# Three plain chunks and six by seven products in the last stage, and earlier sums of the last weights' quarters

## The chip, the cores and the metric

One core of one Trainium2 chip runs the kernel. The metric is the time of one execution in microseconds (us) on the device, the median of several runs. Engine names: PE is TensorE, ACT is ScalarE, DVE is VectorE, POOL is GpSimd, SP is SyncE, which here only issues DMAs.

## What is computed

Memory attention for 4 batches, 8 heads, 576 tokens gives 2304 tokens of 512 features. Two feed-forward blocks follow, and the change lies in the second matmul of the second:

```python
x = (x @ w_a) * (x @ w_b) @ w_out          # first block, d_ff = 1536
h = x @ w_in                               # second block, d_ff = 2048
g = h * (1.0 / (1.0 + np.exp(-1.702 * h)))
return g @ w_out                           # 2304 x 2048 by 2048 x 512, float32
```

## The kernel before

**Precision.** Matmuls run on float32 data cut into a high part, which ScalarE makes by a copy with rounding, and a low part, which VectorE or GpSimd makes by subtracting the high one (`hi_lo`, lines 342 to 346). Each product is three passes: high by high, low by high, high by low (`PASSES`, line 18).

**Seven products.** Most matmul stages multiply two-by-two blocks with seven products (P1 to P7) in place of eight. Each product takes one block of the left side, or a sum of blocks, and one of the right side, and the results are added up afterwards. `PRODUCTS` (line 1063) names the operands; the right side's sums of four quarter blocks are T1 to T4.

**The last stage**, `g @ w_out`, begins at 550.67 us. The gated rows g lie in DRAM (`g2d`), transposed, and the 2304 tokens are cut into nine chunks of 256 (`NW`). Chunks 0 to 2 (`NF`) are computed together, interleaved, by plain products (`proj2`, lines 1467 to 1488): for each quarter of the 2048 contraction rows, for each of six sub-tiles of 128 tokens, four 128-row pieces by three passes, 512 columns each. So 72 matmuls make a quarter. Chunk 3 (from `NF` up to `NQ` = `NS` = 4) follows by plain products alone, two sub-tiles. Chunks 4 to 8 go through `proj2_seven` (lines 1496 to 1521): for each product in the order P4, P1, P2, P5, P7, P6, P3 (`LAST`), two halves (`h`) of the contraction rows, each four pairs of row pieces by three passes, 256 columns each.

**Left side.** `load_gated` (line 1359) issues the loads of g from DRAM on SP: quarters of a chunk of 512 KB into the slots `f_s` (the twelve of chunks 0 to 2, then the four of chunk 3), then halves of 1024 KB into the slots `fw_s`, which use the same memory and are given out once all quarters are split (the mark `"front"`, line 1194). `split_gated` (line 1377) makes high and low parts of each quarter and sub-tile in one of six slots `sb_s`; PE's use of a slot gives it back. For a seven-product chunk `sums_gated` (line 1410) also makes the sums S1 to S4 and splits seven operands a half into the same six slots.

**Right side.** The 16 pieces (128 x 512) of `w_out` come in as raw 64-bit words and are decoded: two ACT instructions and one on DVE (lines 437 to 446). Then ACT copies the high part (line 460), ACT's queue stores the decoded rows in DRAM (`w2d`, line 461) and DVE or POOL makes the low part (line 463). The plain products need piece c = 4q to 4q + 3 in quarter q. The seven products need sums of quarters too: `load_pair` (line 1438) reads two row pieces back from `w2d` on ACT's queue, makes four sums of 128 x 256 in place, one after the other, the last being T4, and splits each (`split_t`, line 1463). There are eight pairs. Two slots for them (`tb_s`, line 1184) exist from the start, and the two raw buffers join once everything is decoded (line 1193).

**What sets the order.** The program is straight-line per engine; the order of instructions on each engine and queue is fixed beforehand by a small planner (`Order`, lines 105 to 192). The work is written as streams with a rank (a lower number goes first). Each stream asks for an engine with a start time and a length, or waits for a mark (a planned time) or a slot; the planner takes the request that can start first, and the lower rank among equals. On the chip each engine then runs in this order and waits by semaphores for the data alone. So an engine whose next instruction, or whose next DMA issue, waits holds everything behind it. `PT` = 28 is the rank of the pair streams, `PR` = 30 that of the decodes of `w_out`; the gated splits have 4 and the gated sums 5. In line 1450 a pair's sums wait, in the planner, for the mark `"decoded"`, which line 1192 sets after the last low part of `w_out`:

```python
t = max((yield "mark", "pair", p), (yield "mark", "decoded"))
```

`proj2_seven` waits, for its first chunk, for the marks of all pairs (lines 1498 to 1500).

Of the kernel before, what the change touches and what calls it, by code (L numbers as in the profile page):

```python
# [22 lines left out]
W1 = 0.0  # L23
HOLD = {}
PR = 30
PT = 28
MBN = 8
PA = 10
HOLDD = {4: ("attn", 1, 0)}
# [42 lines left out]
def short():  # L72
    Lengths.dve, Lengths.act, Lengths.psum = 68, 94, 52
    Lengths.pool, Lengths.both, Lengths.slow = 1.0, 1.0, 1.0
# [121 lines left out]
def tile_mem_attention_moe_moe2(  # L196
# [18 lines left out]
    NT, DM = out.shape  # L215
    F1 = w_o1.shape[0]
    F2 = w_o2.shape[0]
    P = 128
# [19 lines left out]
    K4 = F2 // P // 4  # L238
    NB = 2 * P
# [109 lines left out]
    loaded = {}  # L349
# [62 lines left out]
    decoded = {}  # L412
# [350 lines left out]
    def give(slots_, views):  # L763
        slots_.free += [[x, now()] for x in views]
# [296 lines left out]
    A11, A12, A22, S1, S2, S3, S4 = range(7)  # L1061
# [11 lines left out]
    win_s, hb_s, f_s, fw_s, sb_s, tb_s = Slots(), Slots(), Slots(), Slots(), Slots(), Slots()  # L1073
    wo2_t, blocks = {}, []

    def views(m, n, count, o=0):
        return [m[:, o + i * n:o + (i + 1) * n] for i in range(count)]
# [82 lines left out]
    def room_chunks(*flat):  # L1160
        for x in flat:
            od.mark(now(), "room", "o2", len(wo2))
            wo2.append(x.rearrange("p (i f) -> p i f", i=2))
# [4 lines left out]
    def room_last():  # L1168

        short()  # L1170
        od.handicap[DVE] = W1
        room_chunks(*views(big["w1b"], CN, 2, 3 * CN))
        for x, o, n in (
            (big["w1b"], 5 * CN, 4), (attn_m[0], 0, 9), (p2_rest[0], 0, 5), (attn_m[1], 4 * CN, 1),
            (big["w1"], 0, 14),
        ):
            blocks.extend(x.rearrange("p (i f) -> p i f", i=2) for x in views(x, BN, n, o))
        for q in order:
            for j in range(2):
                for u in range(2):  # L1180
                    yield "mark", "g2", q, j, u
        n = KD * 2 * N2
        give(f_s, views(acc, FN, 1, n + 2 * FN))
        give(tb_s, views(acc, 2 * DM, 2))
        for p in range(F2 // P // 2):
            od.spawn(PT, load_pair(p))
        for c, x in enumerate(views(acc, FN, 2, n), len(pieces) - 3):
            yield "mark", "raw", c
            give(f_s, [x])
        t = yield "mark", "wo2", F2 // P - 1  # L1190
        crowded()
        od.mark(t, "decoded")
        give(tb_s, [x[0].rearrange("p f j -> p (f j)").bitcast(F32) for x in raw_t])
        yield "mark", "front"
        wide = views(acc, 2 * FN, 3, n)
        give(fw_s, wide[:2])
        yield "mark", "sw", NQ, 0, A22
        give(fw_s, wide[2:])
        for p in range(F2 // P // 2):
            yield "mark", "wt", p  # L1200
        short()
        give(fw_s, views(acc, 2 * FN, 1))
        for x in raw_t:
            give(dm_s, views(x[0].rearrange("p f j -> p (f j)").bitcast(F32), DM, 2))
# [133 lines left out]

    NF, NQ, NS, NW = 3, 4, 4, NT // NB

    def gated_part(s, i, o, e):
        t = 0.0
# [9 lines left out]
        loaded["f", i, o] = s, f  # L1354

    QUARTERS = [(i, o) for o in range(0, 4 * K4, K4) for i in range(NF)]
    QUARTERS += [(i, o) for i in range(NF, NQ) for o in range(0, 4 * K4, K4)]

    def load_gated():
        for i, o in QUARTERS:  # L1360
            s = yield "slot", f_s
            yield from gated_part(s, i, o, o + K4)
        for i in range(NQ, NW):
            for o in (0, 2 * K4):
                s = yield "slot", fw_s
                yield from gated_part(s, i, o, o + 2 * K4)

    def split_part(t, src, *key):
        b = yield "slot", sb_s
        loaded[key] = b  # L1370
        od.spawn(4, split_into(max(t, b[1]), b, src, key))
# [5 lines left out]
    def split_gated():  # L1377
        for i, o in QUARTERS:
            t = yield "mark", "f", i, o
            slot, f = loaded.pop(("f", i, o))  # L1380
            for s in range(2):
                yield from split_part(t, f[:, :, s * P:(s + 1) * P], "sb", i, o, s)
            for s in range(2):
                t = max(t, (yield "mark", "sb", i, o, s))
            f_s.release(slot, t)
        od.mark(t, "front")
        for i in range(NQ, NW):
            yield from (split_whole(i) if i < NS else sums_gated(i))

    def split_whole(i):  # L1390
        for h in (0, 2 * K4):
            t = yield "mark", "f", i, h
            slot, f = loaded.pop(("f", i, h))
            for o in range(0, 2 * K4, K4):
                for s in range(2):
                    yield from split_part(t, f[:, o:o + K4, s * P:(s + 1) * P], "sb", i, h + o, s)
            for o in range(0, 2 * K4, K4):
                for s in range(2):
                    t = max(t, (yield "mark", "sb", i, h + o, s))
            fw_s.release(slot, t)  # L1400

    A21 = 7
    MERGE = {
# [34 lines left out]
    def load_pair(p):  # L1438

        t = max((yield "mark", "w2d", 2 * p), (yield "mark", "w2d", 2 * p + 1))  # L1440
        for x in blocks[4 * p:4 * p + 4]:
            wo2_t.setdefault(p, []).append(x)
        m = yield "slot", tb_s
        x = m[0].rearrange("p (k j f) -> p k j f", k=2, j=2)
        nc.scalar.dma_start(
            out=x.rearrange("p k j f -> p k (j f)"),
            in_=w2d[2 * p * P:(2 * p + 2) * P, :].rearrange("(k p) f -> p k f", p=P),
        )
        od.load(max(t, m[1]), 2 * P * DM * 4, "pair", p)
        t = max((yield "mark", "pair", p), (yield "mark", "decoded"))  # L1450
        b11, b12, b21, b22 = (x[:, k, j] for k in range(2) for j in range(2))
        n = DM // 2
        for i, (dst, in0, in1) in enumerate(
            ((b11, b12, b11), (b12, b22, b12), (b22, b22, b11), (b21, b21, b22))
        ):
            t = yield from combine(t, dst, in0, in1, ALU.subtract, n)
            od.spawn(PT, split_t(t, wo2_t[p][i], dst, p, i))
        for i in range(4):
            t = max(t, (yield "mark", "wt", p, i))
        tb_s.release(m, t)  # L1460
        od.mark(t, "wt", p)
# [33 lines left out]

    def proj2_seven(i):

        if i == NS:
            for p in range(2 * K4):
                yield "mark", "wt", p  # L1500
        ps, ts = {}, {}
        for name in LAST:
            a, b = PRODUCTS[name]
            for h in (0, 2 * K4):
                t = yield "mark", "sw", i, h, a
                x = loaded.pop(("sw", i, h, a))
                if h == 0:
                    t, ps[name] = yield PE, t, 360 * K4, bank_m
                else:
                    t, _ = yield PE, t, 360 * K4  # L1510
                for c in range(K4):
                    for n, (mv, sw) in enumerate(PASSES):
                        nc.tensor.matmul(  # L1513
                            ps[name][0][:, :NB], x[0][:, sw, c, :], moving(b, h // 2 + c, mv),
                            start=(h == c == n == 0), stop=(h > 0 and c == K4 - 1 and n == 2),
                        )
                sb_s.release(x, t)
            ts[name] = t
            od.mark(t, "done", i, name)
            if name == LAST[0]:  # L1520
                od.spawn(0, sums_out(i, ps))
# [65 lines left out]
    def main():  # L1587
        yield from all_gated()
        od.spawn(9, part_again())
        room_gated()  # L1590
        crowded()
        for p in range(NP):
            yield from project(p)
        yield from quad(*order[0])
        od.rate, od.land = 385.0, 2000.0
        room_projected()
        od.spawn(6, load_gated())
        od.spawn(5, split_gated())
        for q in order[1:]:
            yield from quad(*q)  # L1600
            if q == (NG2 - 1, 0):
                room_chunks(*views(eff_m, CN, 6), *views(attn_m[1], CN, 4))
            if q == (NG2 - 1, 1):
                room_split(*views(big["w1"], SN, 6, 14 * WN))
                room_chunks(*views(big["w1"], CN, 1, 14 * WN + 6 * SN), *views(big["w1b"], CN, 3))
        od.spawn(9, room_last())
        yield from proj2([(i, s) for i in range(NF) for s in range(2)])
        for i in range(NF, NW):
            yield from (proj2([(i, 0), (i, 1)]) if i < NS else proj2_seven(i))

    def quad(g, p):
        for name in ("P1", "P6", "P7", "P5", "P3", "P4", "P2"):
# [2 lines left out]
    with tc.manual_schedule():  # L1615
# [19 lines left out]
        for n in range(NU):  # L1635
            p = 10 + n if n >= NHG else 10 + PC * n
# [44 lines left out]
```

## Time and profile before

| | |
|---|---|
| median of three runs | 745.47 us (744.72 to 747.44) |
| profiled execution | 744.51 us |
| span of its instructions | 742.7 us |
| PE busy | 732.1 us, 99% |
| DVE, ACT, POOL busy | 533.2, 430.8, 386.1 us |
| mean granted PE clock | 0.999 of full speed |

The profile is of one execution. Its span runs from the first to the last instruction; 1.81 us of the execution's time lie around it. Busy time of an engine is the sum of its instructions; matmuls overlap each other, so a matmul's own duration is longer than the spacing between two of them. In a row of a group the number behind the bar is the sum in us, then the mean in ns of one instruction, then idle time ahead of them with what ended it. Row texts such as `w<-acc,w` name the output and the inputs by their tiles: `w` is the memory of the six split slots, among others, `acc` that of the loaded chunks, `raw` the raw buffers.

### The profile page before, as it was taken

How to read it: one execution, taken by the hardware profiler on the slowest of the kernel's cores; microseconds unless marked ns; L12 is line 12 of the kernel's file. 1: busy time of each engine (PE TensorE's matmuls, PEld its weight loads, DVE VectorE, ACT ScalarE, POOL GpSimd, SP SyncE). 2: the span in 40 equal slices, each digit the busy share in tenths (PEclk: the TensorE clock that was granted, in tenths of full speed). 3: DMA queues.
4: the chain of work that ended last, by engine and by line, in shares of the span. 5: the costliest groups of instructions: out<-in, count | busy, mean ns of one | idle time of the engine just before them, and what ended most of it. 6: DMA issues, size and time to landing. Idle time of an engine off the chain costs nothing.

```text
span 742.7 us, 14507 instructions
## 1 busy us (share of the span) xinstructions
PE 732.1 (99%) x5344; PEld 682.7 (92%) x5344; DVE 533.2 (72%) x799; ACT 430.8 (58%) x842; POOL 386.1 (52%) x347
## 2 busy tenths in 40 slices
PE   9899999999999999999999999999999999999997
PEld 8787888888889999999999999999998888999997
DVE  2987777568983447945898666666665697898884
ACT  3678664667863456546866655565656654544441
POOL 0324366447996616914998621333240296776660
PEclk9999999999999999999999999999999999999999
DMA  8998954786778966676525575544699954544411
GB/s 276 343 327 254 322 190 160 224 280 231 256 237 264 313 195 170 171 211 191 186 100 163 180 227 162 163 136 150 210 377 301 328 157 138 189 143 143 143 26 33
DMA packets 110359, 153.53 MB, mean 207 GB/s; under 512 B 8400, under 2 KB 89040, under 8 KB 110288
## 3 DMA queue, kind: packets, MB, share of 16 engines
q1 hardware_dynamic: 104928, 143.13, 60.3%
q10 hardware_dynamic: 5360, 9.47, 3.9%
q8 instruction: 42, 0.69, 0.4%
q14 instruction: 29, 0.24, 0.1%
HBM read 100.01 MB, written 52.56 MB: 205 GB/s over the span
## 4 chain that ended last, share of the span: by engine, by line
PE 92%; DMA 3%; POOL 2%; DVE 2%; SPq 1%; issue 0%; ACT 0%; DVEq 0%; POOLq 0%
PE bank L1281 24%; PE bank L844 21%; PE bank L1006 16%; PE bank L1513 14%; PE bank L1482 12%; PE bank L792 3%; DMA q<-in_q_dram 1%; PE bank L590 1%; DMA raw_p<-in_moe_w_b_dram 1%; DMA kv<-in_k_dram 1%; PE bank L509 1%; POOL w L339 1%; SPq L372 1%; POOL attn L339 1%; DVE attn L339 0%
## 5 line engine op out<-in xcount | busy, mean ns | idle before, releaser
L844 PEld LDWEIGHTS bank<-attn,eff 128*128 128x128 f32 x1152 | 154.3, 188 | 16.2 <-issue 6.1
L844 PE MATMUL bank<-attn,eff 128*128 128x288 f32 x1152 | 163.1, 298 | 0.5 <-DVE eff L812 0.5
L339 POOL TENSOR_TENSOR acc<-acc 128x512 f32<-128x512 f32 (+2 forms) x65 | 95.0, 1481 | 68.2 <-DVE w L339 27.9
L1323 DVE TENSOR_TENSOR acc<-bank,acc 128x384 f32<-128x384 f32 x168 | 89.8, 553 | 46.3 <-PE bank L1281 40.8
L339 DVE TENSOR_TENSOR w<-acc,w 128x512 fp32r<-128x512 f32 (+2 forms) x100 | 105.0, 1076 | 20.5 <-ACT w L345 20.4
L345 ACT ACTIVATE w<-acc 128x512 fp32r<-128x512 f32 (+2 forms) x129 | 74.9, 590 | 65.7 <-PE bank L1513 38.9
L345 ACT ACTIVATE attn<-acc 128x768 fp32r<-128x768 f32 (+2 forms) x80 | 61.0, 769 | 54.5 <-PE bank L1006 38.7
L1006 PE MATMUL bank<-attn,w 128*128 128x384 f32 x504 | 91.8, 335 | 0.8 <-DVE attn L339 0.7
L1006 PEld LDWEIGHTS bank<-attn,w 128*128 128x128 f32 x504 | 87.5, 188 | 2.0 <-DVE attn L339 1.4
L339 DVE TENSOR_TENSOR attn<-acc,attn 128x768 fp32r<-128x768 f32 (+2 forms) x54 | 65.6, 1225 | 31.9 <-ACT attn L345 30.8
L1333 ACT ACTIVATE acc<-acc 128x384 f32<-128x384 f32 x96 | 49.3, 524 | 44.0 <-DVE acc L1323 43.0
L339 POOL TENSOR_TENSOR attn<-acc,attn 128x768 fp32r<-128x768 f32 (+2 forms) x26 | 41.9, 1623 | 35.8 <-ACT attn L345 35.8
L1281 PE MATMUL bank<-attn,w 128*128 128x384 f32 x288 | 55.1, 334 | 0.0
L339 POOL TENSOR_TENSOR w<-dm,w 128x256 fp32r<-128x256 f32 x27 | 24.5, 908 | 57.9 <-ACT w L345 57.9
L888 POOL TENSOR_TENSOR gr<-gr 128x288 f32<-128x288 f32 x48 | 44.6, 931 | 17.0 <-issue 7.0
L339 POOL TENSOR_TENSOR w<-acc,w 128x256 fp32r<-128x256 f32 (+2 forms) x27 | 30.0, 1119 | 44.4 <-ACT w L345 44.3
L1281 PEld LDWEIGHTS bank<-attn,w 128*128 128x128 f32 x288 | 50.4, 188 | 0.0
L1006 PE MATMUL bank<-attn,w1b 128*128 128x384 f32 x252 | 47.6, 336 | 0.2 <-DVE attn L339 0.2
L339 POOL TENSOR_TENSOR sT<-sT,sm 128x576 f32<-128x576 f32 (+1 forms) x12 | 13.5, 1126 | 64.0 <-DVE sm L654 31.7
L1281 PE MATMUL bank<-w1b,w 128*128 128x384 f32 x224 | 46.2, 334 | 0.0
L1006 PEld LDWEIGHTS bank<-attn,w1b 128*128 128x128 f32 x252 | 43.8, 188 | 0.9 <-DVE attn L339 0.5
L1281 PE MATMUL bank<-w 128*128 128x384 f32 x224 | 43.8, 334 | 0.0
(185 smaller groups left out, 1448.9 us busy)
## 6 DMA issues: line engine op xcount, KB each, us to landing
acc<-g1d SPq DMA_DIRECT2D x63, 384.0 KB, 3.8
g2d<-acc SPq DMA_DIRECT2D x96, 192.0 KB, 2.0
raw<-in_moe_w_out_dram SPq DMA_DIRECT2D x24, 512.0 KB, 4.9
acc<-g2d SPq DMA_DIRECT2D x10, 1024.0 KB, 7.6
raw<-in_moe_w_in_dram SPq DMA_DIRECT2D x16, 512.0 KB, 4.3
acc<-g2d SPq DMA_DIRECT2D x16, 512.0 KB, 5.5
g1d<-gr SPq DMA_DIRECT2D x12, 576.0 KB, 4.9
g1d<-acc SPq DMA_DIRECT2D x8, 576.0 KB, 4.8
```

The costliest lines, as they stand in the source:

```text
L339: (nc.gpsimd if e == POOL else nc.vector).tensor_tensor(out=dst, in0=in0, in1=in1, op=op)
L345: nc.scalar.activation(out=hi, in_=src, func=AF.Copy)
L372: nc.sync.dma_start(out=dst.rearrange("p (n f) w -> p n (f w)", n=runs), in_=src)
L792: nc.tensor.matmul(ps[c][0][row(h), :], bdv[b][half, h, :], wt["wab", g, h][0][half, :], start=True, stop=True)
L844: nc.tensor.matmul(dst[:, :U], e[:, c, sw, i * CW + j * P:i * CW + (j + 1) * P], attn(b, mv, c, u * U, U), start=(n == 0), stop=(n == 3 * ...
L888: nc.gpsimd.tensor_tensor(out=dst, in0=in0, in1=in1, op=ALU.subtract)
L1006: nc.tensor.matmul(ps[0][:, :N2], w1_of(a, g, sw)[:, r * P:(r + 1) * P], b[0][:, mv, i], start=(first and q == n == 0), stop=(q == NG1 // ...
L1281: nc.tensor.matmul(ps[0][:, :N2], w[:, sw, r, :], y[mv][r], start=(n == 0), stop=(n == 5))
L1323: nc.vector.tensor_tensor(out=s[0], in0=ps[0][:, :N2], in1=x[0], op=ALU.add)
L1333: nc.scalar.activation(out=c[0], in_=c[0], func=AF.Gelu_apprx_sigmoid)
L1482: nc.tensor.matmul(ps[i, s][0], b[0][:, sw, c - o, :], wo2[c][:, mv], start=(c == n == 0), stop=(c == 4 * K4 - 1 and n == 2),)
L1513: nc.tensor.matmul(ps[name][0][:, :NB], x[0][:, sw, c, :], moving(b, h // 2 + c, mv), start=(h == c == n == 0), stop=(h > 0 and c == K4 - ...
```

## The change

The constants `NQ` and `NS` go, so chunk 3 is treated as chunks 4 to 8 are: loaded in two halves once the quarters of chunks 0 to 2 are split, summed, and multiplied by seven products. Three chunks are plain and six go by seven products. The pair sums no longer wait for `"decoded"` in the planner, only for their own rows from DRAM, and their rank becomes 31, behind the decodes' 30. `split_whole` had no work before and is removed.

```diff
@@ -23,7 +23,7 @@
 W1 = 0.0
 HOLD = {}
 PR = 30
-PT = 28
+PT = 31
 MBN = 8
 PA = 10
 HOLDD = {4: ("attn", 1, 0)}
@@ -1194,7 +1194,7 @@
         yield "mark", "front"
         wide = views(acc, 2 * FN, 3, n)
         give(fw_s, wide[:2])
-        yield "mark", "sw", NQ, 0, A22
+        yield "mark", "sw", NF, 0, A22
         give(fw_s, wide[2:])
         for p in range(F2 // P // 2):
             yield "mark", "wt", p
@@ -1338,7 +1338,7 @@
 
 
 
-    NF, NQ, NS, NW = 3, 4, 4, NT // NB
+    NF, NW = 3, NT // NB
 
     def gated_part(s, i, o, e):
         t = 0.0
@@ -1354,13 +1354,12 @@
         loaded["f", i, o] = s, f
 
     QUARTERS = [(i, o) for o in range(0, 4 * K4, K4) for i in range(NF)]
-    QUARTERS += [(i, o) for i in range(NF, NQ) for o in range(0, 4 * K4, K4)]
 
     def load_gated():
         for i, o in QUARTERS:
             s = yield "slot", f_s
             yield from gated_part(s, i, o, o + K4)
-        for i in range(NQ, NW):
+        for i in range(NF, NW):
             for o in (0, 2 * K4):
                 s = yield "slot", fw_s
                 yield from gated_part(s, i, o, o + 2 * K4)
@@ -1384,20 +1383,8 @@
                 t = max(t, (yield "mark", "sb", i, o, s))
             f_s.release(slot, t)
         od.mark(t, "front")
-        for i in range(NQ, NW):
-            yield from (split_whole(i) if i < NS else sums_gated(i))
-
-    def split_whole(i):
-        for h in (0, 2 * K4):
-            t = yield "mark", "f", i, h
-            slot, f = loaded.pop(("f", i, h))
-            for o in range(0, 2 * K4, K4):
-                for s in range(2):
-                    yield from split_part(t, f[:, o:o + K4, s * P:(s + 1) * P], "sb", i, h + o, s)
-            for o in range(0, 2 * K4, K4):
-                for s in range(2):
-                    t = max(t, (yield "mark", "sb", i, h + o, s))
-            fw_s.release(slot, t)
+        for i in range(NF, NW):
+            yield from sums_gated(i)
 
     A21 = 7
     MERGE = {
@@ -1447,7 +1434,7 @@
             in_=w2d[2 * p * P:(2 * p + 2) * P, :].rearrange("(k p) f -> p k f", p=P),
         )
         od.load(max(t, m[1]), 2 * P * DM * 4, "pair", p)
-        t = max((yield "mark", "pair", p), (yield "mark", "decoded"))
+        t = yield "mark", "pair", p
         b11, b12, b21, b22 = (x[:, k, j] for k in range(2) for j in range(2))
         n = DM // 2
         for i, (dst, in0, in1) in enumerate(
@@ -1495,7 +1482,7 @@
 
     def proj2_seven(i):
 
-        if i == NS:
+        if i == NF:
             for p in range(2 * K4):
                 yield "mark", "wt", p
         ps, ts = {}, {}
@@ -1606,7 +1593,7 @@
         od.spawn(9, room_last())
         yield from proj2([(i, s) for i in range(NF) for s in range(2)])
         for i in range(NF, NW):
-            yield from (proj2([(i, 0), (i, 1)]) if i < NS else proj2_seven(i))
+            yield from proj2_seven(i)
 
     def quad(g, p):
         for name in ("P1", "P6", "P7", "P5", "P3", "P4", "P2"):
```

## Rows read from the trace of the kernel before

**Rows 1.** The page: span, busy shares, PE's slices and granted clock
```profile
span 742.7 us, 14507 instructions
...
PE 732.1 (99%) x5344; PEld 682.7 (92%) x5344; DVE 533.2 (72%) x799; ACT 430.8 (58%) x842; POOL 386.1 (52%) x347
...
PE   9899999999999999999999999999999999999997
...
PEclk9999999999999999999999999999999999999999
```

**Rows 2.** The chain that ended last: start us, us, what; its end
```profile
375.95 174.72 PE bank L1281 x1008
550.67 87.08 PE bank L1482 x384
637.75 100.80 PE bank L1513 x840
738.58 0.42 DVE raw L1541
```

**Rows 3.** Windows: busy us (instructions) of each engine, PE clock, DMA share, GB/s
```profile
550.67:562.00 11.33, 11.33 (x51) 9.34 (x51) 3.19 (x7) 4.71 (x10) 0.00 (x0) 1.00 1.00 319
562.00:587.00 25.00, 25.00 (x112) 20.71 (x111) 15.16 (x24) 16.41 (x29) 0.90 (x1) 1.00 0.98 342
587.00:616.00 29.00, 29.00 (x129) 24.01 (x129) 26.41 (x33) 16.92 (x42) 25.58 (x28) 1.00 0.60 177
616.00:637.75 21.75, 21.75 (x98) 18.01 (x98) 14.14 (x17) 8.62 (x17) 10.53 (x11) 1.00 0.68 205
637.75:657.91 20.16, 20.16 (x170) 20.16 (x170) 19.32 (x20) 9.71 (x17) 16.16 (x11) 1.00 0.49 155
```

**Rows 4.** Groups by line and shape, one seven-product chunk, 657.91 to 678.07 us
```profile
L339 DVE TENSOR_TENSOR w<-acc,w 128x512 fp32r<-128x512 f32 x14 | 16.2, 1182 | 2.7 <-ACT w L345 2.7
L339 POOL TENSOR_TENSOR acc<-acc 128x512 f32<-128x512 f32 x9 | 14.6, 1643 | 6.6 <-DVE w L339 6.6
L345 ACT ACTIVATE w<-acc 128x512 fp32r<-128x512 f32 x15 | 9.5, 631 | 11.0 <-PE bank L1513 9.7 <-DVE w L339 0.8 <-POOL acc L339 0.5
...
L1513 PEld LDWEIGHTS bank<-attn,w 128*128 128x128 f32 x48 | 6.3, 192 | 0.0
...
L1541 DVE TENSOR_TENSOR raw<-bank,raw 128x256 f32<-128x256 f32 x5 | 2.0, 413 | 0.0
```

**Rows 5.** Timeline of VectorE around 587 and 607 us: start us, us, what
```profile
586.96 0.69 DVE L339 TENSOR_TENSOR w1b<-acc,w1b 128x512 fp32r<-128x512 f32 x1
587.57 0.42 DVE L339 TENSOR_TENSOR acc<-acc 128x256 f32<-128x256 f32 x1
...
607.16 0.95 DVE L339 TENSOR_TENSOR w<-acc,w 128x512 fp32r<-128x512 f32 x1 [0.90 <-ACT w L345]
```

**Rows 6.** Timeline of GpSimd: first, second and last stretch of the quarter sums
```profile
562.32 0.90 POOL L339 TENSOR_TENSOR acc<-acc 128x256 f32<-128x256 f32 x1 [12.57 <-DMA acc<-w2d]
588.12 1.44 POOL L339 TENSOR_TENSOR acc<-acc 128x256 f32<-128x256 f32 x2 [24.91 <-DVE acc L339]
...
620.66 3.82 POOL L339 TENSOR_TENSOR w<-raw,w 128x256 fp32r<-128x256 f32 x4
```

**Rows 7.** The 128x512 subtractions, 562 to 587 us (first), 590 to 620 (second)
```profile
L339 DVE TENSOR_TENSOR w<-acc,w 128x512 fp32r<-128x512 f32 x10 | 7.3, 739 | 0.0
...
L339 DVE TENSOR_TENSOR w<-acc,w 128x512 fp32r<-128x512 f32 x10 | 11.1, 1109 | 2.6 <-ACT w L345 2.6
```

**Rows 8.** Ns min/median/max of line 1445's waits; landing of line 461's stores
```profile
L1445 ACTq EVENT_SEMAPHORE  x9: 17/38/3898, 552.4 to 606.6; - x9
...
DMA to landing us min/median/max: 2.1/4.9/6.6
```

**Rows 9.** Timeline of ScalarE, three reads' followers, with idle time before each
```profile
600.62 0.63 ACT L345 ACTIVATE w<-acc 128x512 fp32r<-128x512 f32 x1 [1.47 <-DVE w1b L339]
...
602.05 0.63 ACT L345 ACTIVATE w<-acc 128x512 fp32r<-128x512 f32 x1 [0.80 <-POOL attn L339]
...
606.50 0.63 ACT L345 ACTIVATE w<-acc 128x512 fp32r<-128x512 f32 x1 [3.82 <-DVE acc L339]
```

**Rows 10.** Groups of ScalarE, 562 to 587 us: what the decodes wait for
```profile
L438 ACT ACTIVATE dm<-raw 128x512 f32<-128x512 f32 x4 | 2.7, 663 | 4.6 <-DMA raw<-in_moe_w_out_dram 4.6
...
L438 ACT ACTIVATE acc<-raw 128x512 f32<-128x512 f32 x2 | 1.3, 666 | 2.8 <-DMA raw<-in_moe_w_out_dram 2.8
```

**Rows 11.** Timeline of SyncE's queue: quarter loads, output stores, half loads
```profile
579.24 16.65 SPq L1350 DMA_DIRECT2D acc<-g2d  x4
609.24 7.42 SPq L1568 DMA_DIRECT2D out_dram<-dm  x12
...
626.26 5.25 SPq L1350 DMA_DIRECT2D acc<-g2d  x4
```

**Rows 12.** First copy (ScalarE) and first subtraction (VectorE) of chunk 4's half
```profile
631.80 1.15 ACT L345 ACTIVATE w<-acc 128x512 fp32r<-128x512 f32 x2 [9.35 <-DMA acc<-g2d]
...
632.47 0.69 DVE L339 TENSOR_TENSOR w<-acc,w 128x512 fp32r<-128x512 f32 x1 [6.23 <-ACT w L345]
```

## The prediction

> **What bounds the kernel now.** I read the page's busy shares first: PE is busy 732.1 of the 742.7 us span, at a granted clock that never leaves its upper level (2.4 GHz) [rows 1]. Then the chain that ended last: from 375.95 us it holds nothing but PE, first the gating stage, then 87.08 us of plain second-projection matmuls (384) and 100.80 us of seven-product ones (840), and one VectorE addition behind the last of them [rows 2]. So in the stage the change touches, time is the number of matmuls times their spacing, and every other engine matters only if it makes PE wait. Last I read the windows table, which shows what stands beside PE: in the 65.3 us of the first three plain chunks (550.67 to 616) VectorE is busy 44.8 us and GpSimd 26.5, and GpSimd does nearly nothing before 587 [rows 3].
>
> **The change part by part.**
>
> *Matmuls.* One plain matmul of 512 columns takes 87.08/384 = 226.8 ns, one of 256 columns 100.80/840 = 120.0 ns [rows 2]. A plain chunk has 2 sub-tiles x 16 contraction chunks x 3 passes = 96 of them, 21.77 us; a seven-product chunk has 7 x 8 x 3 = 168, 20.16 us. One chunk changes its kind: **-1.61 us**, all on the path. Nothing else is saved, since PE has no gap in this stage to win back.
>
> The saving is small because a seventh fewer multiply columns (49152 become 43008) is bought with 72 more instructions. From the two spacings: 226.8 - 120.0 = 106.8 ns for 256 columns, so 13.2 ns of each matmul is fixed; 72 more of them give back 0.95 of the 2.56 us. The Trainium skill (TensorE: Matmul & The Clock Gate, section Back-to-back issue gap) speaks against the change: it puts a sustained pair of weight load and matmul at about 81 ns for 128 columns and 131 ns for 512. On a straight line between them 256 columns would take some 98 ns (an estimate from that page), and the chunk would go from 12.6 to 16.4 us, 3.8 us slower. This trace contradicts both figures: 120.0 and 226.8 ns over hundreds of matmuls.
>
> *Work beside PE for the chunk.* Plain: 8 ScalarE copies, 8 low-part subtractions, 2 evictions. Seven products: 14 copies at 0.63 us, 14 subtractions at 1.18 us, 8 sums at 1.64 us, 7 additions out of PSUM at 0.41 us [rows 4]. In the seven-product stage of before, the chunk from 637.75 shows VectorE 19.32 and GpSimd 16.16 us busy in 20.16 us and PE is full all the same [rows 3]. The sixth such chunk costs 0 while its inputs are there in time.
>
> *The wait on all decodes goes.* The 32 quarter sums, 32 copies and 32 subtractions stay the same in number. Before, the first sum starts at 562.32 us, the second only at 587.57, right behind the subtraction of the last plain weight piece (586.96), and the last subtraction ends at 620.66 + 3.82 = 624.5 us [rows 5, 6]. Products now begin at 616.0 instead of 637.75. The first one, P4, reads T4 of the last pair in its last three matmuls, at 616.0 + 21 x 0.120 = 618.5 us. So the sums must come at least 6.0 us earlier, and they have an almost empty GpSimd from 562 to do it in. A bill for the stretch up to 616: now 71.2 us on the two engines; with everything that both now do between 616 and 637.75 added, 24.7 us, an upper bound for the rest of the sums and for the first products' inputs, it is 95.9 of 130.6 us [rows 3]. It fits at 73%. Cost taken: 0; without that room, what the third rival gives.
>
> *What the earlier sums slow.* A 128x512 subtraction takes 0.74 us where GpSimd is idle and 1.11 us where it works beside it [rows 7]. All 15.16 us of VectorE's work between 562 and 587 stretched by 1.5 would be 22.7 of 25 us [rows 3]: it still fits. Between nothing and 7.6 us of VectorE time, I take the upper end; on PE it costs 0.
>
> *Eight reads on ScalarE's queue.* The pair reads move between the decodes. A read waits in ScalarE's order for the landing of the rows' store (median 4.9, up to 6.6 us) and for its slot, and all that stands behind it waits too: decodes, and the copies that feed PE. Waits of that kind cost 3.9 us at most before [rows 8]; ScalarE idled 1.47, 0.80 and 3.82 us behind three of the last reads [rows 9]. Six reads (pairs 2 to 7) come among or close behind the decodes; bounds 0 and 6 x 3.9 = 23.4 us of ScalarE, I take the mean of those three, 2.0 each, 12.2 in all. Of this 7.4 us replaces time in which the decodes wait for their own loads anyway [rows 10]. The reads also load the transfer engines, 98% busy there at 342 GB/s [rows 3]: 6 x 0.52 MB is 9.2 us more, and the four quarter loads of chunk 3 that leave the stretch are 6.1 us less, so 3.1 us. Together the last weight piece, now done at 586.96 + 0.69 = 587.7 [rows 5], comes 7.9 us later. PE reads it first at 550.67 + 3 x 16.33 + 9 x 0.227 = 601.7, a cover of 14.0 us. Cost 0; without that cover, the excess.
>
> *Chunk 3's loads.* Four quarter loads that queue at 579.24 to 596 become two half loads that wait until the last three-chunk piece is split. Before, that split ends at 607.16 + 0.95 = 608.1 us, 3.8 us of it due to a pair read ahead of it [rows 5, 9]. From issue to the first copy of such a half took 626.26 to 631.80, 5.5 us, and to the end of the first subtraction 1.4 us more [rows 11, 12]. Worst case 608.1 + 6.9 = 615.0, without that pair read about 611: just before the 616.0 at which PE wants it. Bounds 0 and the 7.5 us worked out under the second rival; taken 0, being nearer to these rows.
>
> **Sum:** -1.61 + 0. The profiled execution (744.51 us, of which 1.81 lie around the span) would become 742.90; the median of the runs shown, 745.47, stands 0.96 above it, so the forecast is 745.47 - 1.61 = **743.9 us**. That is 0.2%, less than the 0.5% (3.7 us) a measurement of this kernel can tell from no change.
>
> **Rivals.**
>
> *ScalarE held by pair reads* (slower). Place: the last quarter of the plain chunks, from 599.7. If the six reads cost the full 3.9 us each, the last weight piece is 23.4 - 14.0 = 9.4 us late: 753.3 us. It decides above 2.3 us a read, and counts as slower above 749.2 us, at 3.2 a read. For it: with transfers that full, stores land late. Against: ScalarE itself is busy only 16.4 of those 25 us.
>
> *Chunk 3's halves queue behind output stores* (slower). SyncE issues in order; the first twelve stores hold it from 609.24 to 616.7 [rows 11]. Were the half loads behind them: 616.7 + 6.9 = 623.5, 7.5 us late, 751.4 us; behind the first four, 2.6 us late, 746.5. Against: the loads' condition comes before any tile of the last quarter is evicted.
>
> *The sums don't really move* (the change does not do what it says): the two slots are reused slowly, or the lowest rank keeps the sums last. Then the last split ends at 624.5 as now, 6.0 us after P4 wants it: 749.9 us. Against: in 562 to 587 nothing else wants GpSimd.
>
> *Narrow matmuls bound by their weight loads.* PE's loads are busy all of the seven-product stage but 83% of the plain one [rows 3]. At a load's 192 ns apiece [rows 4] the chunk would take 32.3 us, 10.5 more: 756.0. The 120.0 ns of [rows 2] leave this next to nothing. The rule of the TensorE page of the Trainium skill cited above would give 749.3 in its place; the trace disagrees with it.
>
> **How the numbers follow.** Forecast 0.76, held ScalarE 0.08, loads behind stores 0.06, sums not moved 0.05, narrow matmuls 0.01, anything else 0.04, half of it a gain that I don't see. Above 749.2 I put half of the first two rivals, nearly all of the third, and the fourth: slower 0.12. Faster by over 0.5% needs 2 us of gain from a stage with no gap: 0.02. The rest, 0.86, is within. The runs before spread 0.75 below and 1.97 us above their median, which round 743.9 gives 743.1 to 745.8; with a wait of 1.4 us from the rivals above that, and 0.4 us below for a spacing a little better than worked out, the range is 742.7 to 747.2.
>
> **What would show it.** Right: 288 plain matmuls at 226.8 ns and 1008 at 120.0, no gap on PE between, together 186.3 us instead of 187.9; the last quarter split before 616; sums on GpSimd from 562; pair reads among the decodes. Wrong: a PE wait at 599.7 to 602 on a weight piece, at 616 on a copy of the chunk's half, or at 618 on a quarter split; or a spacing other than these two.

## The result, and the profile after

The changed kernel takes 751.73 us (median of 10 runs, 749.35 to 753.95), the kernel before 746.24 us beside it (10 runs). The ratio is 1.0081, 95% interval 1.0066 to 1.0096: **5.5 us slower by the medians** (0.8%), where 1.6 us faster was forecast; the range ended at 747.2. One run of all, of 2535.59 us with early halves and late sums, took over three times as long as its sisters and is left out of medians and ratios. The profiled execution took 750.37 us with a span of 748.5 us, against 744.51 and 742.7 before.

The page's head, as in [rows 1]:

```profile
span 748.5 us, 14700 instructions
...
PE 734.0 (98%) x5416; PEld 686.4 (92%) x5416; DVE 541.4 (72%) x824; ACT 434.2 (58%) x847; POOL 388.8 (52%) x343
```

PE runs 72 more matmuls, as worked out, and is busy 98% instead of 99%. The chain of waits that ended last (start us, us, what) shows where it was not:

```profile
551.05 8.22 PE bank L1469 x36
...
597.55 2.01 DMA w2d<-acc
...
612.78 0.36 SPq L1350
613.23 7.67 DMA acc<-g2d
620.92 1.51 DMA out_dram<-dm
622.43 0.63 ACT w L345
623.10 121.41 PE bank L1500 x996
```

In [rows 2] the chain is PE alone from 375.95 us on. Here it leaves PE in the plain part, goes through decodes, pair reads, quarter sums and splits, and comes back at 623.10, after a load of chunk 3 (`acc<-g2d`, asked for at 612.78 us), an output store and a copy on ScalarE. PE's own timeline at the switch, with the idle time before each group in brackets:

```profile
606.72 10.91 PE L1469 MATMUL bank<-w1b,w 128*128 128x512 f32 x46 [0.57 <-DVE w L339]
618.72 0.50 PE L1500 MATMUL bank<-w1b,w 128*128 128x256 f32 x2 [1.09 <-ACT w L345]
...
623.10 3.22 PE L1500 MATMUL bank<-w 128*128 128x256 f32 x12 [2.20 <-ACT w L345]
```

and the windows table (PE, PEld, DVE, ACT, POOL busy; clock; transfers):

```profile
616.40:618.00 1.60, 1.24 (x6) 0.70 (x4) 0.00 (x0) 0.00 (x0) 0.00 (x0) 1.00 1.10 364
...
620.00:622.00 2.00, 0.90 (x8) 0.70 (x6) 1.10 (x1) 0.07 (x1) 0.55 (x1) 1.00 0.93 313
622.00:624.00 2.00, 0.90 (x3) 0.68 (x4) 0.92 (x2) 2.00 (x5) 0.15 (x1) 0.76 0.44 106
624.00:626.00 2.00, 2.00 (x10) 2.00 (x11) 2.00 (x3) 1.61 (x4) 2.00 (x2) 0.50 0.61 140
626.00:628.00 2.00, 2.00 (x17) 2.00 (x17) 2.00 (x3) 0.79 (x2) 2.00 (x2) 0.89 1.08 383
```

Between 616.4 and 618 VectorE, ScalarE and GpSimd stand still and PE ends its last plain matmuls, while the transfers run at 364 GB/s. From the start of the stage, 551.05, the matmuls alone would end 65.31 + 120.96 us later, at 737.3; the last addition starts at 744.5. The missing **7.2 us**: the last plain matmul starts at 617.2 where 550.89 + 287 x 0.2268 = 615.98 was due (1.2); PE waits for the copy of P4's first half (1.3); P4's first twelve matmuls take 0.6 too long, waiting for the low part; it waits for the second half (2.4); and the last 996 matmuls take 121.41 us instead of 119.52 and the 0.16 by which the last of them outlasts the spacing (1.7), while the granted clock falls to 0.50, the lower level of 1.2 GHz, after PE's idle time.

Why was chunk 3 asked for so late? Its halves wait for the last split of the first three chunks. VectorE and SyncE's queue:

```profile
598.21 1.00 DVE L339 TENSOR_TENSOR w1b<-acc,w1b 128x512 fp32r<-128x512 f32 x1 [0.36 <-ACT w1b L460]
...
610.38 2.38 DVE L339 TENSOR_TENSOR w<-acc,w 128x512 fp32r<-128x512 f32 x2
```
```profile
612.78 0.98 SPq L1350 DMA_DIRECT2D acc<-g2d  x2
613.86 9.73 SPq L1555 DMA_DIRECT2D out_dram<-dm  x12
623.63 1.08 SPq L1350 DMA_DIRECT2D acc<-g2d  x2
```

The last weight piece is ready at 599.2 us (587.7 in [rows 5]), the last split at 612.76 (608.1 there), and the half loads follow at once. ScalarE's timeline has the pair reads between its copies; what follows a read shows the wait:

```profile
569.68 0.68 ACT L438 ACTIVATE dm<-raw 128x512 f32<-128x512 f32 x1 [1.29 <-POOL w1b L339]
...
576.84 0.73 ACT L345 ACTIVATE attn<-acc 128x256 fp32r<-128x256 f32 x2 [1.79 <-POOL attn L339]
...
580.20 0.67 ACT L438 ACTIVATE dm<-raw 128x512 f32<-128x512 f32 x1 [0.39 <-DVE attn L339]
...
590.00 0.73 ACT L345 ACTIVATE rest<-acc 128x256 fp32r<-128x256 f32 x2 [1.52 <-DVE acc L339]
...
594.52 0.63 ACT L460 ACTIVATE w1b<-dm 128x512 fp32r<-128x512 f32 x1 [1.53 <-POOL attn L339]
...
600.12 2.47 ACT L345 ACTIVATE w<-acc 128x256 fp32r<-128x256 f32 x7 [1.42 <-POOL acc L339]
```

The first five of these reads wait for a slot, which the subtractions of an earlier pair, on GpSimd and VectorE, have to free. The last, ahead of the copy at 600.12, waits for the store of the last rows, which the chain shows landing 2.01 us after 597.55.

### The profile page after: what moved, and what is told of

Same layout as the page of the kernel before. It is cut to its first block, busy times and chain, and to the rows that moved or that the text cites. A ratio compares the mean times of both kernels' runs of the same rounds, so it can differ in the third digit from the quotient of the medians.

```text
span 748.5 us, 14700 instructions
## 1 busy us (share of the span) xinstructions
PE 734.0 (98%) x5416; PEld 686.4 (92%) x5416; DVE 541.4 (72%) x824; ACT 434.2 (58%) x847; POOL 388.8 (52%) x343
## 4 chain that ended last, share of the span: by engine, by line
PE 84%; DMA 6%; DVE 4%; issue 2%; ACT 2%; POOL 1%; SPq 0%; ACTq 0%; DVEq 0%; POOLq 0%
PE bank L1281 23%; PE bank L844 21%; PE bank L1500 16%; PE bank L1006 16%; PE bank L792 3%; DMA raw<-in_moe_w_out_dram 1%; DVE w L339 1%; PE bank L1469 1%; DMA acc<-g2d 1%; PE bank L590 1%; DMA raw_p<-in_moe_w_b_dram 1%; DMA kv<-in_v_dram 1%; DMA kv<-in_k_dram 1%; DVE attn L339 1%; PE bank L509 1%
## 5 line engine op out<-in xcount | busy, mean ns | idle before, releaser
L339 POOL TENSOR_TENSOR acc<-acc 128x512 f32<-128x512 f32 (+2 forms) x72 | 107.9, 1521 | 63.1 <-DVE w L339 34.6
L339 DVE TENSOR_TENSOR w<-acc,w 128x512 fp32r<-128x512 f32 (+2 forms) x109 | 114.2, 1076 | 20.9 <-ACT w L345 20.8
L345 ACT ACTIVATE w<-acc 128x512 fp32r<-128x512 f32 (+2 forms) x139 | 80.0, 586 | 65.6 <-PE bank L1500 44.3
L345 ACT ACTIVATE attn<-acc 128x768 fp32r<-128x768 f32 (+2 forms) x85 | 62.8, 748 | 58.0 <-PE bank L1006 39.9
L339 DVE TENSOR_TENSOR attn<-acc,attn 128x768 fp32r<-128x768 f32 (+3 forms) x61 | 69.7, 1152 | 32.2 <-ACT attn L345 30.8
L339 POOL TENSOR_TENSOR attn<-acc,attn 128x768 fp32r<-128x768 f32 (+2 forms) x24 | 40.1, 1681 | 43.6 <-ACT attn L345 38.5
```

The source lines that it names most:

```text
L339: (nc.gpsimd if e == POOL else nc.vector).tensor_tensor(out=dst, in0=in0, in1=in1, op=op)
L345: nc.scalar.activation(out=hi, in_=src, func=AF.Copy)
```

## The experiments

The two parts were first run apart, then each suspected cause was removed. With each edit the planner places other instructions anew too, so a run can differ in more than the cause it names; its trace has to show the wait that it is about. Beside all of them ran the kernel before, at 746.35 to 746.74 us.

**Sevens alone** (the sums as before):

```diff
-PT = 31
+PT = 28
...
-        t = yield "mark", "pair", p
+        t = max((yield "mark", "pair", p), (yield "mark", "decoded"))
```

> The changed kernel with the pair sums as before (rank 28, waiting in the planner for the last decode), so only chunk 3's change of kind is left. Theory S (switch): in the changed kernel the pair reads among the decodes hold ScalarE, the last weight piece is done 11.6 us later (599.2 instead of 587.7), the rest of the pair sums collide with the last quarter's splits, chunk 3's half loads are issued at 612.8 only, and PE idles and then runs some 6 us at half clock. It expects here: last weight piece at 588 +- 1, half loads issued by 609, and in their place late quarter sums (last pair's subtraction at 620 to 624); 747 to 750 us. Rival R (the sevens themselves: halves that can be asked for only after the last split are late whatever the pair sums do) expects the changed kernel's time again, 751 to 753 us, with PE waiting on the copy of chunk 3's half.

Measured 755.29 us, ratio 1.013 (1.0101 to 1.0159). The half loads came at 608.20, as theory S said, but the time is above both expectations. PE's timeline:

```profile
620.74 0.50 PE L1500 MATMUL bank<-w 128*128 128x256 f32 x2 [1.90 <-ACT w L345]
...
625.97 0.58 PE L1500 MATMUL bank<-w 128*128 128x256 f32 x1 [3.41 <-ACT w L345]
```

and ScalarE's before the first of these:

```profile
619.57 0.60 ACT L330 ACTIVATE dm<-bank 128x512 f32<-128x512 f32 x1 [2.08 <-DMA out_dram<-dm]
620.06 1.66 ACT L345 ACTIVATE w<-acc 128x512 fp32r<-128x512 f32 x3
```

The first wait is for the copy of the chunk's second half, which stands behind an eviction that waits for an output store, as in the changed kernel. The second, the longest, is P4's matmul with T4 of the last pair, whose subtraction starts at 625.95 us on VectorE. So early sums are needed for a sixth seven-product chunk: without them it costs 8.9 us, with them 5.5. Against the stage's start the half loads come at 57.4 us, where the last split ended before the change too, and at 61.7 in the changed kernel: the earlier sums are what delays them there.

**Sums alone** (the kernel before with `PT = 31` and without the wait for `"decoded"`; four plain chunks):

> The kernel before with the early pair sums alone (rank 31, no wait for the last decode), four plain chunks. Theory S: the decodes are late here too, last weight piece at about 599, PE held by under 1.5 us in the last quarter of the three plain chunks, but chunk 3 comes in quarters loaded early, so no idle time at 617 and none at the switch to seven products; 746 to 748 us, PE's clock at its upper level throughout. Rival R expects no loss, 746.2 +- 0.7, and decodes as before (588). A third reading, that the early sums alone cost the whole 6 us, expects 751 to 753 us.

Measured 749.72 us, ratio 1.0047 (1.0029 to 1.0065): 3.4 us lost without any change of chunk 3, more than theory S allowed, and not what R said. ScalarE's timeline in the last quarter, then PE's:

```profile
600.78 0.33 ACTq L461 DMA_DIRECT2D w2d<-acc  x1
601.32 0.61 ACT L345 ACTIVATE w<-acc 128x512 fp32r<-128x512 f32 x1
605.61 0.38 ACTq L1445 DMA_DIRECT2D raw<-w2d  x1
606.03 1.46 ACT L345 ACTIVATE w<-acc 128x512 fp32r<-128x512 f32 x3 [4.10 <-DMA w2d<-acc]
```
```profile
606.71 12.26 PE L1482 MATMUL bank<-w1b,w 128*128 128x512 f32 x50 [1.35 <-ACT w L345]
619.73 2.57 PE L1482 MATMUL bank<-w1b,w 128*128 128x512 f32 x10 [0.76 <-DVE w L339]
```

By the spacing of 226.8 ns PE loses 1.9 us ahead of the first of these rows and 1.7 between the two, where low parts come late. The read of the last pair stands close behind the store of the last rows; ScalarE waits 4.10 us for this store to land, and the copy behind the read is the one that PE wants at 605. The Trainium skill (DMA: Bandwidth & Descriptors, section Two DMAs through the same engine are not ordered) asks for this wait: the second DMA may be issued only when the first has reported completion; here it was, 4.83 us after the store. It is the place of the read in the order that is dear, not the wait as such.

**Reads on GpSimd's queue** (`nc.gpsimd.dma_start` in `load_pair`):

> The changed kernel with the eight pair reads issued from GpSimd's queue instead of ScalarE's. Theory S: ScalarE no longer waits for the reads, the last weight piece is done by 592, the last quarter's last split by 609, PE's idle time around the switch falls from 4.3 us to under 2 us; 745 to 748 us, unless GpSimd, which now waits for the reads, delays the sums. Rival R: 751 to 753 us, since the halves are asked for after the last split all the same.

Measured 755.26 us, ratio 1.0128 (1.0105 to 1.0152): worse, the exception that the expectation names. GpSimd now waits in ScalarE's place, sums come late, VectorE waits for them, and PE for VectorE:

```profile
611.69 14.76 PE L1469 MATMUL bank<-w1b,w 128*128 128x512 f32 x58 [4.04 <-DVE w L339]
```

**Two pairs early, six after the last decode**:

```diff
+        if p >= 2:
+            yield "mark", "decoded"
         m = yield "slot", tb_s
```

> The changed kernel, but only the first two pairs are read and summed early; the other six reads wait in the planner for the last decode. Theory S: two reads among the decodes as in the kernel before, so the last weight piece at 588 to 590; six pairs of sums are left from there, done by 616; half loads issued by 609; 745 to 748 us. Rival R: 751 to 753 us.

Measured 756.71 us, ratio 1.0139 (1.0106 to 1.0172): theory S missed by 9 us. The decodes are on time (last weight piece at 590.6), but six pairs' sums then lie in front of the last quarter's splits and the half loads come even later:

```profile
615.89 0.98 SPq L1350 DMA_DIRECT2D acc<-g2d  x2
```
```profile
621.98 0.51 PE L1502 MATMUL bank<-w1b,w 128*128 128x256 f32 x2 [3.50 <-ACT w L345]
```

PE's longest wait is for the copy of the first half. So decodes on time do not help while the half loads are late. That led to theory H.

**Halves early.** Chunk 3's halves go into the memory of quarters that are split long before the last one:

```diff
-        yield "mark", "front"
-        wide = views(acc, 2 * FN, 3, n)
-        give(fw_s, wide[:2])
-        yield "mark", "sw", NF, 0, A22
-        give(fw_s, wide[2:])
+        od.spawn(9, halves_early(views(acc, 2 * FN, 3, n)))
...
+    def halves_early(wide):
+        yield "mark", "sb", 1, 2 * K4, 1
+        give(fw_s, wide[1:2])
+        yield "mark", "sb", 1, 3 * K4, 1
+        give(fw_s, wide[2:])
+        yield "mark", "front"
+        yield "mark", "sw", NF, 0, A22
+        give(fw_s, wide[:1])
```

> The changed kernel, but chunk 3's two halves are loaded as soon as the quarters whose memory they use are split (the second quarter row of chunk 1, the last one of chunk 1), not after the last split of all. Theory H (half loads): of the changed kernel's loss, the idle time of PE around the switch (4.3 us) and the half clock after it (1.9 us) come from the late half loads, and the rest, under 1 us, from late splits in the last quarter. It expects no wait over 0.5 us at the switch, the clock at its upper level, and 751.7 - 6.2 = 745.5 us (744.5 to 747). Rival C (crunch): ScalarE, VectorE and GpSimd are full up to 612 whatever is loaded, so the halves' splits only take the place of the pair sums and PE waits for these instead; 750 to 753 us.

Measured 746.28 us (12 runs), ratio to the kernel before 0.9997 (0.9984 to 1.001): the loss of 5.5 us is gone, but nothing is gained. The chain's last rows and one of PE's timeline:

```profile
606.10 13.68 PE bank L1474 x58
619.77 120.96 PE bank L1505 x1008
```
```profile
606.10 13.68 PE L1474 MATMUL bank<-w1b,w 128*128 128x512 f32 x58 [0.47 <-DVE w L339]
```

All 1008 narrow matmuls now run without a gap at 120.0 ns, and the granted clock stays at its upper level. This execution's stage began at 552.9 us, so the plain part still lasts 66.9 us instead of 65.3: the saving of 1.6 us is eaten by waits in the last quarter.

**Halves early, sums late** (the same on top of the first run):

> The same early half loads, with the pair sums as before the change (rank 28, after the last decode). Theory H says that two inputs of the first seven-product chunk are each late by themselves: halves as well as quarter sums, so this waits for the last pair's T4 as the run with sevens only did (ready at 626): 752 to 755 us, PE idle before the second half of P4. Rival C expects about the sevens-only time too, 755 us, or more. If this comes out at 745 to 747, the early sums were needless.

Measured 754.65 us (three runs), ratio 1.0125 (1.0102 to 1.0148), PE held by pair copies again:

```profile
626.47 0.58 PE L1505 MATMUL bank<-w 128*128 128x256 f32 x1 [3.63 <-ACT w L345]
```

Halves and quarter sums are two inputs of the same first product, and each holds PE alone.

**Reads when due.** The planner resumes a stream as soon as a mark is known, even if its time lies ahead, so a read was put into ScalarE's order before its rows had landed or its slot was free. Three runs hold it back until the planner's ScalarE clock has come there: with early halves, on the changed kernel, and on the sums alone.

```diff
         m = yield "slot", tb_s
+        t = max(t + 2500.0, m[1])
+        yield "when", lambda: t if od.clock[ACT] >= t else None
```

> The run with early half loads, and each pair read put into ScalarE's order only where the planner's ScalarE clock has reached the time at which the rows (5 us after their store) and the slot are there; so far a read was put in at once, and ScalarE waited in its place. Theory Q (queue): the 1.5 us that the early halves left on the table (plain part 66.85 us instead of 65.31) are ScalarE's waits at the reads, 1.3 to 1.9 us each, ahead of the last quarter's splits. It expects no wait of ScalarE over 0.5 us at a read, the plain part at 65.3 to 65.8 us, and 744.8 us (744 to 746), ratio 0.998. Rival V (VectorE and GpSimd): they are simply full from 597 to 612, and moving the reads changes nothing: 746.3 again, plain part over 66.5 us.

> The changed kernel with the reads put in when due, half loads as late as in it. Theory Q: last split of the last quarter at 608 to 610 instead of 612.8, so the half loads come 3 to 5 us sooner and PE's idle time falls by about as much: 747 to 749.5 us. Rival V: the changed kernel's time, 751 to 753 us.

> Four plain chunks, early sums, reads put in when due. Theory Q: the loss of the sums alone (749.7) is ScalarE waiting at the reads ahead of the last quarter's splits, so it is gone: 746.5 us (745.5 to 747.5). Rival V: 749 to 751 us.

Measured, with early halves: **745.23 us** (12 runs), ratio 0.9975 (0.9964 to 0.9987), as theory Q said. Sums alone: 746.37 us, ratio 0.9998 (0.9986 to 1.0011), and PE has no wait left in its last quarter, so the 3.4 us of the second run came from these reads' places. The changed kernel: 750.91 us, ratio 1.0056 (1.0033 to 1.0078), a miss for Q: the halves come at 613.37 in a stage that began 2.0 us later, so only 1.4 us sooner, and the idle time at the switch stays. Of the 4.3 us that the half loads came later than the last split of before, the reads' places thus explain 1.4. The chain of the sums alone, then of the version with early halves:

```profile
552.47 87.08 PE bank L1484 x384
```
```profile
550.80 65.32 PE bank L1476 x288
616.12 120.96 PE bank L1507 x1008
```

and one of the latter's reads on ScalarE, no longer followed by a wait:

```profile
600.78 0.38 ACTq L1439 DMA_DIRECT2D raw<-w2d  x1
601.20 1.15 ACT L345 ACTIVATE w<-acc 128x512 fp32r<-128x512 f32 x2
```

The version with early halves beats both kernels, the kernel before by a quarter of a percent, with the whole interval below 1.

## Why the prediction was wrong

- *Matmuls, -1.61 us.* Right, as the last version shows: 65.32/288 = 226.8 ns and 120.96/1008 = 120.0 ns, 186.28 us in place of 187.88, and 745.23 us against 746.74 beside it. So narrow matmuls keep a spacing below the 192 ns of a weight load [rows 4].
- *Chunk 3's loads, cost taken 0.* **This step failed.** It took the last split's end of before, 608.1 us, as the worst case, though the same text moved quarter sums in front of it that had come behind it (15 of their 32 copies, with their subtractions). It came at 612.76; with the sums as before it came as early as before. Then 5.5 us from issue to copy was read from one half; the second of two halves landed at 620.9, 8.1 us after 612.78. The trace of before already had this: its four half loads issued from 626.26 on landed 5.4 to 11.8 us after issue. And the copy behind it stood in ScalarE's order after an eviction that waited for an output store of its buffer, another 1.5 us. PE got P4's second half at 623.1 where 617.4 had been expected. The run with early halves shows that this step is worth about 5.5 us, with the clock's share below.
- *The clock* had no term: idle time was priced at its own length, and 1.7 us came on top.
- *Reads on ScalarE's queue.* The waits were taken too long, on the safe side: in the changed kernel the six reads cost 7.9 us in all (12.2 taken). The last weight piece came 11.2 us later against the stage's start (7.9 taken) and still in time for 601.7. What was not followed is the other thing said to stand behind a read, the copies that feed PE: 1.2 us in the changed kernel, 3.4 us in the sums alone.
- *The bill of VectorE and GpSimd* was right and answered the wrong question: 48.0 + 24.2 us were used by 616.4, 55% of the room, and yet the last split was late. In a fixed order two engines that are idle nearly half the time can still be late.
- *The earlier sums* came as said, the last at 612.2 us for 618.5, and the third rival was wrong. The first had the right place for a smaller loss. The second came within a microsecond of the time, 751.4, by luck: the halves were ahead of the stores in SyncE's order, but late, and it was an eviction that stood behind a store. Both together had 0.14.

## What to carry to other kernels

A stage that is shortened takes cover from everything that was due behind it: list each input of the first instruction that now comes sooner, and follow each back to what *asks* for it, since here the load was only issued after work that the same change had delayed. A bound taken from the old trace is no bound for an instruction that gets new neighbours on its engine. And a DMA that reads back what a queue has just stored belongs in the order where the store has landed, not behind its issue.

## What was unexpected of the hardware

In the changed kernel PE was busy 3.2 of the 6.7 us from 616.4 to 623.1:

```profile
616.40:623.10 6.70, 3.19 (x18) 2.24 (x17) 2.38 (x3) 2.80 (x6) 1.28 (x1) 1.00 0.92 296
```

The granted clock was then 0.76 in 622 to 624, 0.50 in 624 to 626, 0.89 in 626 to 628 and 1.00 after that, and the matmuls in it lost 1.7 us. In windows of 1 us from 623 to 627 it was 0.52, 0.50, 0.50 and 0.78, so the lower level held for less than the 6 us named in the first expectation. With the sevens alone, where PE stood for longer, it was at 0.50 from 624 to 632. So the 4.3 us that PE stood at the switch (1.3, 0.6 and 2.4) cost 1.7 us on top here. Two 1 MB loads issued together took 8.1 us until the second had landed, with the transfers at 313 to 364 GB/s from 616.4 to 622.
